# Attention's places in the first MoE's tiles spread wider, two more raw weight buffers, and the second MoE's first splits cut into pieces

## The chip, the cores and the metric

The kernel runs on one core of one Trainium2 chip. The metric is the device time of one execution in microseconds. Three runs of the kernel before gave 1160.42, 1161.3 and 1163.42 us; the median is 1161.3 us. Five engines work side by side, each through its own queue in order: TensorE (PE, with its weight loads PEld), VectorE (DVE), ScalarE (ACT), GpSimdE (POOL) and SyncE (SP, which here only issues DMAs).

## The reference

The input is a chunked attention (4 batches, 8 heads, 768 places, head width 64, chunks of 32 queries that see their own 32 places, 16 before, 8 behind and 8 memory places). Its output is 3072 rows of 512, and two mixtures of matrix products follow. All of it is float64 on the host or float32 on the chip.

```python
scores = scale * np.matmul(q_c, k_full.transpose(0, 1, 3, 2))
a = np.exp(scores - np.max(scores, axis=-1, keepdims=True))
a = a / (np.sum(a, axis=-1, keepdims=True) + 1e-09)
out[:, :, c_start:c_end] = np.matmul(a, v_full)
...
xn = x / rms * rms_g                       # first MoE, 512 -> 1536 -> 512
g = xn @ w_gate
h = g * (1.0 / (1.0 + np.exp(-g))) * (xn @ w_val)
x2 = h @ w_out
...
h = x2 @ w_in                              # second MoE, 512 -> 2048 -> 512
g = np.where(h >= 1, h, np.where(h <= -1, 0.0, (h + 1) ** 2 / 4))
y = g @ w_out
```

## The kernel before, in words

Every large product is done with each operand split into a high part and a low rest, both in a 32-bit matmul format, and three matmuls for each product (high x high, high x low, low x high). The rows are cut into six tiles of 512 (`TT`).

**Start.** Four units of attention (a unit is half of a pair of 128-row blocks) fill the first tile. `ORDER` writes that order out by hand: `s` scores, `m` and `e` softmax, `a` transposes of the exponentials, `A` their copy to SBUF, `v` product with the values, `n` division, `q`, `k`, `p`, `r` the row scaling, `x` transposes of the result, `c`, `d`, `g`, `o` the four steps that turn one raw weight into its two parts.

**First MoE, tiles t = 0 to 3**, one at a time. Each tile has twelve blocks f. A block is 12 matmuls of 512 columns for the gate (`proj_in` into `ps_g[0]`), 12 for the value (into `ps_g[1]`), 12 for the block before's output (`out1` into `ps_y`). After each of the three stands a slot, `slot(t, 3f)`, `slot(t, 3f+1)`, `slot(t, 3f+2)`: 36 slots in a tile. A slot may hold one step of attention for the tiles to come (`att_slot`: the table `plan` in tile 0, `plan2` and `plan3` in tiles 1 to 3, where a pair of units takes 11 slots), and some of the background work: in tile 0 `conv_w` and `load_w` (the 36 raw weights, 512 KB each, by way of the three buffers of `wst`), later `conv_step`, which makes the sums of weights that the second half needs. In the tiles of 1 and 2 `load_x` fetches the next tile's x (1 MB) at f = 9, and `split_x` splits it at f = 11. Slots 34 of tile 1 and 34 of tile 2 hold no attention. At f = 6 of tile 3 attention is over; its SBUF is given to the tile `y`, and `load_y` fetches tiles 4 and 5. From f = 8 on `x_steps`, twelve small groups of DVE and ACT work, one per slot, turn `y` into the operands of the pair.

In tile 0 PE and SP run in program order, and a scheduler places the instructions of ACT, DVE and POOL; from tile 1 on all engines run in program order. Attention's scores, transposes and products all go through one PSUM bank pair, `ps_a`.

**Pairs.** Tiles 4 and 5 in the first MoE, and all six tiles as three pairs in the second, are done with seven products instead of eight for a 2x2 block. `seven` is one such block of 42 matmuls: product 0 into bank A, product 1 into C, then ACT copies A to B (L891) and C to the tile `p5` (L892), product 2 adds into B, and so on; DVE adds `p5` and B into C (L899) and later into `p5` (L903). In the second MoE `proj2` runs eight such blocks for a pair, each followed by the clamp and square (`clamp`, `top`); then `Out.run` does the output product from splits (`split`: ACT's copy to a high part at L982, DVE's rest at L984, and a sum at L986). The splits of blocks 0 to 3 are made ahead, by `o2.ahead(g - 3)` behind blocks 3 to 6 of the projection. The first of the `x_steps` for the next pair, a DVE sum over 128x1024 (L812), is taken behind block 6.

Of the kernel before, what the change touches and what calls it, by code (L numbers as in the profile page):

```python
# [39 lines left out]
def tile_stream_attention_moe_moe2(  # L40
# [72 lines left out]
    raw, absd, f32s = [], [], []  # L113
# [413 lines left out]
    def step_x(pr, blk, ps):  # L527
# [4 lines left out]
        for kk in range(KK):  # L532
            nc.tensor.transpose(ps[:, 0, kk * P:(kk + 1) * P], x[blk][:, kk * P:(kk + 1) * P], ident)
        ps_t["x", pr, blk] = ps

    def part_X(pr, blk):
# [7 lines left out]
        rows = ps[:, 0, :].rearrange("p (k i) -> p k i", k=KK)  # L544
# [73 lines left out]
    for st in ORDER.split():  # L618
# [5 lines left out]
        if c in "savx":  # L624
            use[c, n] = free.pop(0)
            ps = slots[use[c, n]]
            if c == "x":
                step_x(n // 2, n % 2, ps)
# [31 lines left out]
        elif c == "d":  # L660
            conv_d()
            load_w(units1, 1)
# [15 lines left out]
    plan = {1: "s0", 3: "a0", 4: "v0", 7: "s1", 9: "a1", 10: "v1", 11: "r0", 14: "x0", 15: "x1"}  # L678

    plan2 = {0: "s0", 3: "a0", 4: "s1", 5: "v0", 6: "a1", 8: "v1", 11: "r0", 12: "x0", 13: "x1"}
    plan3 = {0: "s0", 3: "a0", 4: "s1", 5: "v0", 6: "a1", 7: "v1", 9: "r0", 10: "x0", 11: "x1"}

    def att_slot(t, s):
        if t == 0:
            o, r = divmod(s, 18)
            if r in plan:
                att_step(2 + o, plan[r])
            return  # L690

        if s == 34:
            return
        s += 36 * (t - 1)
        s -= (s > 34) + (s > 70)
# [6 lines left out]
    def att_step(pr, st):  # L702
# [3 lines left out]
        if st[0] == "x":  # L706
            step_x(pr, n, ps_a)
# [28 lines left out]
    def slot(t, s):  # L736
# [8 lines left out]
        else:  # L745
# [4 lines left out]
            conv_step(1 if s > 32 else PACE[(n - (n > 34) - (n > 70)) % 11] if n < 92 else 2.5)  # L750
# [74 lines left out]
    for t in range(NS):  # L825
# [3 lines left out]
        for f in range(F1):  # L829
            if 0 < t < NS - 1 and f == 9:  # L830
                load_x(t + 1)
# [9 lines left out]
            if t == NS - 1 and f == 6:  # L841
                att_only.close()
                right = ctx.enter_context(tc.tile_pool(name="right", bufs=1, side="right", reuse_waits="tile"))
                m2["y"] = right.tile([P, 2, KK, TT], F32, name="y")
                load_y(x_d[NS], x_d[NS + 1])
# [13 lines left out]
            slot(t, 3 * f + 2)  # L859
    for i in range(8, 14):  # L860
# [20 lines left out]
    banks, defer = [], []  # L881

    def seven(n, early):
# [7 lines left out]
        nc.scalar.activation(B, A, AF.Copy)  # L891
        nc.scalar.activation(p5, C, AF.Copy)  # L892
# [58 lines left out]
    class Out:  # L951
# [23 lines left out]
        def split(self, n):  # L975
# [9 lines left out]
            if p == 0:  # L985
                tt_(out=B11, in0=B12, in1=B11, op=ALU.add)  # L986

# [261 lines left out]
```

## Time and profile before

| | |
|---|---|
| median of three runs | 1161.3 us |
| the profiled execution | 1158.09 us |
| its span, first to last instruction | 1156.3 us |
| granted TensorE clock, mean | 0.989 |
| PE busy | 1125.6 us (97%) |
| DVE busy | 820.6 us (71%) |
| ACT busy | 617.3 us (53%) |
| bytes moved by DMA | 281.81 MB, 244 GB/s |

The span begins at the first instruction. In microseconds from there, the start takes until 35, tile 0 until 151, tile 1 until 272, tile 2 until 391, tile 3 until 503, the last pair of the first MoE until 676, and the three pairs of the second MoE the rest. A matmul's start tells more than its busy time, since matmuls are pipelined: the time from one start to the next is what the engine spends on one. In the timelines a row's brackets give the idle time of the engine just before it and what ended that; a wait for several things is put down to the one that came last by the trace's record, which may be the wrong one where that engine had long been done.

### The profile page before, as it was taken

What the parts mean: (1) busy time and instruction counts of PE and PEld (TensorE: products, weight loads), DVE (VectorE), ACT (ScalarE), POOL (GpSimd) and SP (SyncE); (2) the same over time, 40 slices, a digit from 0 to 9 for tenths busy, and PEclk for the clock granted to TensorE, in tenths of its full rate; (3) what the DMA queues carried; (4) which work ended last, traced back from release to release, by engine and by line L of the source; (5) the groups of instructions that cost most, each with busy time, mean ns of one, the idle gap of its engine ahead of it and who ended that gap; (6) DMA issues with size and microseconds to landing.
All of it is one profiled execution on the core that took longest, in us unless ns stands there. A gap on an engine that the chain in (4) does not pass through costs nothing.

```text
span 1156.3 us, 20945 instructions
## 1 busy us (share of the span) xinstructions
PE 1125.6 (97%) x7879; PEld 909.7 (79%) x7879; DVE 820.6 (71%) x1433; ACT 617.3 (53%) x1088; POOL 102.6 (9%) x152
## 2 busy tenths in 40 slices
PE   5899999999999999999999999999999999999998
PEld 4677788877788777887888888788887788887886
DVE  3887667767756666766676867897677887578855
ACT  3777665656565765534444634456444465344553
POOL 0200003213222222101110000000000000000000
PEclk7999999999999999999999999999999999999999
DMA  8776448998979887779997697756778666762564
GB/s 294 253 258 203 163 140 271 312 310 284 303 245 309 269 273 236 275 269 383 404 394 241 213 316 246 210 180 199 231 207 260 177 195 216 217 197 86 164 188 158
DMA packets 144212, 281.81 MB, mean 244 GB/s; under 512 B 15216, under 2 KB 65392, under 8 KB 142320
## 3 DMA queue, kind: packets, MB, share of 16 engines
q1 hardware_dynamic: 123664, 228.57, 60.7%
q0 software_dynamic: 12768, 43.52, 10.8%
q10 hardware_dynamic: 7680, 8.39, 2.1%
q8 instruction: 62, 1.02, 0.3%
q14 instruction: 38, 0.31, 0.1%
HBM read 201.26 MB, written 79.17 MB: 243 GB/s over the span
## 4 chain that ended last, share of the span: by engine, by line
PE 76%; DVE 8%; ACT 6%; DMA 6%; issue 3%; POOL 1%; SPq 0%; DVEq 0%; ACTq 0%; POOLq 0%
PE ps_y L1034 14%; PE ps_g L1034 11%; PE ps_g L557 6%; PE ps_g L559 5%; PE ps_g L558 5%; PE ps_g L872 3%; PE ps_b L872 3%; PE ps_b L874 3%; PE ps_b L873 3%; PE ps_g L874 3%; PE ps_g L873 3%; DMA w<-in_w_dram 3%; PE ps_y L557 3%; PE ps_y L558 3%; PE ps_y L559 3%
## 5 line engine op out<-in xcount | busy, mean ns | idle before, releaser
L557 PE MATMUL ps_g<-xh,wall 128*128 128x512 f32 x384 | 156.6, 408 | 3.2 <-ACT wall L152 3.2
L1034 PE MATMUL ps_y<-r,wo 128*128 128x512 f32 x672 | 156.2, 390 | 0.0
L558 PE MATMUL ps_g<-xl,wall 128*128 128x512 f32 x384 | 151.1, 394 | 0.4 <-DVE xl L652 0.4
L559 PE MATMUL ps_g<-xh,wall 128*128 128x512 f32 x384 | 151.3, 394 | 0.2 <-DVE wall L154 0.2
L1034 PEld LDWEIGHTS ps_y<-r,wo 128*128 128x128 f32 x672 | 125.7, 188 | 26.0
L984 DVE TENSOR_TENSOR r<-h,r 128x512 fp32r<-128x512 f32 x167 | 112.2, 689 | 44.0 <-ACT r L982 43.9
L935 ACT ACTIVATE t<-t,half 128x512 f32<-128x512 f32 x96 | 66.9, 720 | 128.4 <-DVE t L934 125.5
L982 ACT ACTIVATE r<-h 128x512 fp32r<-128x512 f32 x167 | 100.4, 624 | 56.2 <-DVE r L984 18.2
L1034 PE MATMUL ps_g<-r,wo 128*128 128x512 f32 x498 | 116.0, 390 | 0.0
L1034 PEld LDWEIGHTS ps_g<-r,wo 128*128 128x128 f32 x498 | 93.2, 188 | 19.4 <-DVE r L984 0.2
L557 PEld LDWEIGHTS ps_g<-xh,wall 128*128 128x128 f32 x384 | 72.8, 190 | 19.6 <-ACT wall L152 3.8
L559 PEld LDWEIGHTS ps_g<-xh,wall 128*128 128x128 f32 x384 | 72.7, 189 | 17.1 <-DVE wall L154 1.0
L558 PEld LDWEIGHTS ps_g<-xl,wall 128*128 128x128 f32 x384 | 73.0, 190 | 14.3 <-DVE xl L652 0.7
L872 PE MATMUL ps_g<-wall 128*128 128x512 f32 x198 | 78.4, 396 | 1.6 <-DVE ps_y L899 0.8
L872 PE MATMUL ps_b<-wall 128*128 128x512 f32 x202 | 79.2, 392 | 0.7 <-DVE ps_g L899 0.3
L873 PE MATMUL ps_b<-wall 128*128 128x512 f32 x202 | 78.6, 389 | 0.0
L874 PE MATMUL ps_b<-wall 128*128 128x512 f32 x202 | 78.6, 389 | 0.0
L557 PE MATMUL ps_y<-hh,wall 128*128 128x512 f32 x192 | 77.9, 406 | 0.0
L873 PE MATMUL ps_g<-wall 128*128 128x512 f32 x198 | 77.1, 390 | 0.0
L874 PE MATMUL ps_g<-wall 128*128 128x512 f32 x198 | 77.1, 389 | 0.0
L558 PE MATMUL ps_y<-hl,wall 128*128 128x512 f32 x192 | 75.2, 392 | 0.0
L559 PE MATMUL ps_y<-hh,wall 128*128 128x512 f32 x192 | 74.9, 390 | 0.0
(199 smaller groups left out, 2086.7 us busy)
## 6 DMA issues: line engine op xcount, KB each, us to landing
wo<-w2o_d SPq DMA_DIRECT2D x88, 512.0 KB, 3.4
wall<-w2p_d SPq DMA_DIRECT2D x168, 256.0 KB, 2.9
wall<-w1p_d SPq DMA_DIRECT2D x84, 256.0 KB, 5.9
w<-in_w_dram SPq DMA_DIRECT2D x36, 512.0 KB, 4.6
w<-in_w_dram POOLq DMA_DIRECT2D x32, 512.0 KB, 5.7
k_in<-in_k_dram SPq DMA_DIRECT2D x48, 256.0 KB, 4.9
wo<-w1o_d SPq DMA_DIRECT2D x21, 512.0 KB, 3.5
v_in<-in_v_dram SPq DMA_DIRECT2D x40, 260.0 KB, 4.3
```

The lines of the kernel that those rows point to most:

```text
L557: nc.tensor.matmul(ps, wh, xh, start=start, stop=False)
L558: nc.tensor.matmul(ps, wh, xl, start=False, stop=False)
L559: nc.tensor.matmul(ps, wl, xh, start=False, stop=stop)
L872: nc.tensor.matmul(bank, wh, xh, start=st, stop=False, skip_group_check=True)
L873: nc.tensor.matmul(bank, wh, xl, start=False, stop=False, skip_group_check=True)
L874: nc.tensor.matmul(bank, wl, xh, start=False, stop=kk == 1, skip_group_check=True)
L935: nc.scalar.activation(s, s, AF.Square, scale=0.5, bias=half)
L982: nc.scalar.activation(r[:, 0], src, AF.Copy)
L984: tt_(out=r[:, 1], in0=src, in1=r[:, 0].bitcast(F32), op=ALU.subtract)
L1034: nc.tensor.matmul(bank[p][m], a, b, start=s0, stop=s1, skip_group_check=True)
```

## The change

It has four parts.

- **Tile 0's weights.** Two more raw buffers (`w64s`) are cut out of the `xn` tile, which tile 0 needs only once attention's third pair is transposed. Of the first 15 raw weights every fourth and fifth goes there; one more load is issued in the start.
- **Attention's places.** In tile 0 the two pairs no longer stand at the same places of two halves of 18 slots; one table gives all 18 places, with two slots or more between `a` and its `v`, and `x0` and `x1` two slots apart. In tiles 1 and 2 slots 33 and 34 (36 + 34 and 36 + 35 in tile 2) hold no attention instead of one slot each, so everything behind them stands one or two slots later; `plan2` scales a pair (`r0`) at 10 instead of 11.
- **Order of loads.** `load_x` stands behind the slot at f = 9 instead of ahead of it; the giving away of attention's SBUF and `load_y` stand behind slot 3f+2 of f = 6 instead of 3f.
- **Second MoE.** The first splits are no longer made behind a block but in pieces inside the next one (`pieces`, `due`): ACT's copy behind the bank copy L891, DVE's rest ahead of the sum L899, DVE's sum behind it. The first of the `x_steps` goes there too, behind the first clamp.

```diff
     def load_w(units, n):
         for _ in range(n):
             if units:
                 dst, key, src = units.pop()
-                w64 = wst.tile([P, 1024], U32, tag="w64", name="w64")
+                i = 3 * F1 - 1 - len(units)
+                if i == 3:
+                    spare.append(xs.tile([P, 2, 1024], U32, tag="xn", name="w64s"))
+                if i < 15 and i % 5 > 2:
+                    w64 = spare[0][:, i % 5 - 3]
+                else:
+                    w64 = wst.tile([P, 1024], U32, tag="w64", name="w64")
                 nc.sync.dma_start(w64, src)
...
             conv_d()
-            load_w(units1, 1)
+            load_w(units1, 1 if n else 2)
...
-    plan = {1: "s0", 3: "a0", 4: "v0", 7: "s1", 9: "a1", 10: "v1", 11: "r0", 14: "x0", 15: "x1"}
-    plan2 = {0: "s0", 3: "a0", 4: "s1", 5: "v0", 6: "a1", 8: "v1", 11: "r0", 12: "x0", 13: "x1"}
+    plan = {
+        2: (2, "a0"), 4: (2, "v0"), 5: (2, "s1"), 7: (2, "a1"), 9: (2, "v1"), 11: (2, "r0"), 12: (2, "x0"), 14: (2, "x1"),
+        16: (3, "s0"), 19: (3, "a0"), 21: (3, "v0"), 22: (3, "s1"), 24: (3, "a1"), 26: (3, "v1"), 29: (3, "r0"),
+        30: (3, "x0"), 32: (3, "x1"),
+    }
+    plan2 = {0: "s0", 3: "a0", 4: "s1", 5: "v0", 6: "a1", 8: "v1", 10: "r0", 12: "x0", 13: "x1"}
...
-        if s == 34:
+        s += 36 * (t - 1)
+        if s in (33, 34, 70, 71):
             return
-        s += 36 * (t - 1)
-        s -= (s > 34) + (s > 70)
+        s -= 2 * (s > 34) + 2 * (s > 71)
...
-            if 0 < t < NS - 1 and f == 9:
-                load_x(t + 1)
...
             slot(t, 3 * f)
-            if t == NS - 1 and f == 6:
-                att_only.close()
-                ...
-                load_y(x_d[NS], x_d[NS + 1])
+            if 0 < t < NS - 1 and f == 9:
+                load_x(t + 1)
...
             slot(t, 3 * f + 2)
+            if t == NS - 1 and f == 6:
+                att_only.close()
+                ...
+                load_y(x_d[NS], x_d[NS + 1])
...
         nc.scalar.activation(B, A, AF.Copy)
+        due(0)
         nc.scalar.activation(p5, C, AF.Copy)
...
         product(7 * n + 3, A, False)
+        due(1)
         tt(out=C, in0=p5, in1=B, op=ALU.add)
+        due(2)
         done11 = early(A)
+        due(3)
...
+        def pieces(self, n):
+            if not 0 <= n < self.L:
+                return
+            p, k, B11, B12, B21, B22 = self.block(n)
+            r = m2["ring"][n % len(m2["ring"])]
+            later2[0].append(lambda: nc.scalar.activation(r[:, 0], B11, AF.Copy))
+            later2[1].append(lambda: tt_(out=r[:, 1], in0=B11, in1=r[:, 0].bitcast(F32), op=ALU.subtract))
+            later2[2].append(lambda: tt_(out=B11, in0=B12, in1=B11, op=ALU.add))
...
             proj2(G2 * pr + g)
-            o2.ahead(g - 3)
+            if g < G2 - 1:
+                o2.pieces(g - 3)
...
             if g == 6 and xq:
-                xq.pop(0)()
+                later2[3].append(xq.pop(0))
```

How the instructions stand on their engines, at three places. In all of them the program's line numbers of the changed kernel are 6 to 28 higher than before.

First, PE in block f = 0 and 1 of tile 0, before (`ps_g_111` is `ps_g[0]`, `ps_g_112` is `ps_g[1]`, `ident,e` the transposes `a0` of unit 4):

```order
L557 MATMUL ps_g_111<-xh,wall 128x512
L558 MATMUL ps_g_111<-xl,wall 128x512
L559 MATMUL ps_g_111<-xh,wall 128x512
L437 MATMUL ps_a<-ident,e 128x128 x4
L557 MATMUL ps_g_112<-xh,wall 128x512
```

and now:

```order
L564 MATMUL ps_g_112<-xl,wall 128x512
L565 MATMUL ps_g_112<-xh,wall 128x512
L443 MATMUL ps_a<-ident,e 128x128 x4
L563 MATMUL ps_g_111<-xh,wall 128x512
L564 MATMUL ps_g_111<-xl,wall 128x512
```

The transposes stood between the gate and the value product of f = 1; they stand now behind the value product of f = 0, 12 matmuls earlier. On ACT the same stretch read before (`tu<-w` is step `c` of a raw weight, `wall<-tu` step `g`, `e<-e` the exponential that the transposes read, with the table load ahead of it):

```order
L152 ACTIVATE wall<-tu 128x512
L128 ACTIVATE tu<-w_587 128x512
L837 ACT_TABLE_LOAD
L837 ACTIVATE s<-ps_g_111 128x512
L152 ACTIVATE wall<-tu 128x512
L432 ACT_TABLE_LOAD
L432 ACTIVATE e<-e 128x512
L128 ACTIVATE tu<-w_669 128x512
```

and now:

```order
L158 ACTIVATE wall<-tu 128x512
L134 ACTIVATE tu<-w64s 128x512 x2
L841 ACT_TABLE_LOAD
L841 ACTIVATE s<-ps_g_111 128x512
L158 ACTIVATE wall<-tu 128x512
L438 ACT_TABLE_LOAD
L438 ACTIVATE e<-e 128x512
L134 ACTIVATE tu<-w_670 128x512
```

Two raw weights instead of one are taken up ahead of the exponential; the one that came behind it (`w_669`) is now the second `w64s`.

Second, SP at f = 9 of tile 1, before (`xn<-x_d` is `load_x`, `v_in` the values of unit 13, `w1p_d` a store of summed weights):

```order
L202 DMA w1p_d_141<-wgv 128x2x256
L202 DMA w1p_d_141<-s_2878 128x2x256
L552 DMA xn<-x_d_119 128x2048
L392 DMA v_in<-in_v_dram 128x520 x2
L202 DMA w1p_d_142<-wgv 128x2x256
```

and now:

```order
L208 DMA w1p_d_141<-wgv 128x2x256
L208 DMA w1p_d_141<-s_2873 128x2x256
L398 DMA v_in<-in_v_dram 128x520 x2
L558 DMA xn<-x_d_119 128x2048
L208 DMA w1p_d_142<-wgv 128x2x256
```

The two loads of the values stand ahead of the load of x.

Third, ACT in the second MoE, pair 0, around the start of block 4, before (`half` marks the square of `clamp`, `r<-h` the split's high part, `ps_g_112<-ps_y_705` the bank copy, the last row but one the copy to `p5`):

```order
L935 ACTIVATE t_7243<-t_7243,half 128x512
L982 ACTIVATE r_7244<-h 128x512
L891 ACTIVATE ps_g_112<-ps_y_705 128x512
L892 ACTIVATE t_7237<-ps_g_111 128x512
L935 ACTIVATE t_7238<-t_7238,half 128x512
```

and now:

```order
L950 ACTIVATE t_7233<-t_7233,half 128x512
L902 ACTIVATE ps_g_112<-ps_y_706 128x512
L1010 ACTIVATE r_7239<-h 128x512
L904 ACTIVATE t_7234<-ps_g_111 128x512
L950 ACTIVATE t_7235<-t_7235,half 128x512
```

The bank copy has come ahead of the split's copy. The same exchange stands in blocks 4 to 7 of each of the three pairs.

## Rows read from the trace of the kernel before

**Rows 1.** The page: span, busy time of each engine with its share and instructions.

```profile
span 1156.3 us, 20945 instructions
PE 1125.6 (97%) x7879; PEld 909.7 (79%) x7879; DVE 820.6 (71%) x1433; ACT 617.3 (53%) x1088; POOL 102.6 (9%) x152
```

**Rows 2.** Waits of PE, whole span: who for whom: us in total, times, longest.

```profile
PE ps_g L557 <- ACT wall L152: 3.2, 2, 1.6
PE ps_a L453 <- ACT aT L443: 2.2, 4, 0.7
PE ps_a L533 <- ACT x_nat L546: 1.8, 4, 0.6
```

**Rows 3.** Timeline of PE, tile 0: start us, us, engine line op tiles xcount [idle].

```profile
36.90 0.40 PE L557 MATMUL ps_g<-xh,wall 128*128 128x512 f32 x1
41.46 0.39 PE L559 MATMUL ps_g<-xh,wall 128*128 128x512 f32 x1
46.61 0.50 PE L557 MATMUL ps_g<-xh,wall 128*128 128x512 f32 x1 [1.59 <-ACT wall L152]
58.42 0.50 PE L557 MATMUL ps_g<-xh,wall 128*128 128x512 f32 x1 [1.56 <-ACT wall L152]
61.02 0.63 PE L558 MATMUL ps_g<-xl,wall 128*128 128x512 f32 x1
61.45 0.63 PE L559 MATMUL ps_g<-xh,wall 128*128 128x512 f32 x1
```

**Rows 4.** Stretches of tile 0: busy by engine, granted clock, DMA share, GB/s.

```profile
30.00:36.00 6.00, 5.20 (x85) 2.94 (x83) 5.46 (x11) 4.40 (x11) 0.69 (x1) 0.77 0.27 90
52.00:58.00 6.00, 4.87 (x22) 3.69 (x20) 4.21 (x13) 3.02 (x9) 2.18 (x3) 1.00 0.93 304
58.00:64.00 6.00, 5.42 (x76) 3.66 (x76) 4.88 (x9) 3.44 (x6) 0.00 (x0) 0.72 0.88 315
```

**Rows 5.** Timeline of ACT, tile 0, columns as in rows 3.

```profile
41.01 1.28 ACT L432 ACT_TABLE_LOAD   x1
42.30 0.63 ACT L432 ACTIVATE e<-e 128x512 f32<-128x512 f32 x1
56.25 0.66 ACT L128 ACTIVATE tu<-w 128x512 f32<-128x512 f32 x1 [1.40 <-DMA w<-in_w_dram]
```

**Rows 6.** Timeline of SP, end of tile 1.

```profile
244.96 1.13 SPq L552 DMA_DIRECT2D xn<-x_d  x1
246.18 1.24 SPq L392 DMA_DIRECT2D v_in<-in_v_dram  x2
```

**Rows 7.** DMA issues of 244 to 248 us: xcount, KB each, us to landing.

```profile
v_in<-in_v_dram SPq DMA_DIRECT2D x2, 260.0 KB, 7.3
```

**Rows 8.** Timeline of PE, end of tile 1.

```profile
253.67 0.35 PE L453 MATMUL ps_a<-v_in,aT 64*32 64x65 f32 x16 [2.35 <-ACT wgv L197]
256.00 0.63 PE L559 MATMUL ps_g<-xh,wall 128*128 128x512 f32 x1
```

**Rows 9.** Timeline of DVE, tile 3.

```profile
469.84 1.23 DVE L812 TENSOR_TENSOR y<-y 128x1024 f32<-128x1024 f32 x1 [0.83 <-DMA y<-x_d]
473.77 0.69 DVE L849 TENSOR_TENSOR s<-s,ps_g 128x512 f32<-128x512 f32 x1 [2.37 <-PE ps_g L559]
```

**Rows 10.** Timeline of ACT, second MoE, pair 0.

```profile
716.28 0.62 ACT L982 ACTIVATE r<-h 128x512 fp32r<-128x512 f32 x1
716.80 0.58 ACT L891 ACTIVATE ps_g<-ps_y 128x512 f32<-128x512 f32 x1
726.74 0.58 ACT L891 ACTIVATE ps_y<-ps_b 128x512 f32<-128x512 f32 x1
```

**Rows 11.** Timeline of PE, second MoE, pair 0.

```profile
716.92 0.39 PE L874 MATMUL ps_g<-wall 128*128 128x512 f32 x1
717.43 0.50 PE L872 MATMUL ps_g<-wall 128*128 128x512 f32 x1
...
750.62 0.50 PE L872 MATMUL ps_g<-wall 128*128 128x512 f32 x1 [0.38 <-DVE ps_y L899]
```

More of the change, by code (lines that the diff above doesn't have):

```diff
@@ L112, in tile_stream_attention_moe_moe2 @@
     w1 = {}
-    raw, absd, f32s = [], [], []
+    raw, absd, f32s, spare = [], [], [], []
     def load_w(units, n):
@@ L532, in step_x @@
         for kk in range(KK):
-            nc.tensor.transpose(ps[:, 0, kk * P:(kk + 1) * P], x[blk][:, kk * P:(kk + 1) * P], ident)
+            nc.tensor.transpose(ps[:, kk * P:(kk + 1) * P], x[blk][:, kk * P:(kk + 1) * P], ident)
         ps_t["x", pr, blk] = ps
@@ L543, in part_X @@
             xn = x_t[pr][blk].rearrange("p (k i) -> p k i", k=KK)
-        rows = ps[:, 0, :].rearrange("p (k i) -> p k i", k=KK)
+        rows = ps.rearrange("p (k i) -> p k i", k=KK)
         for kk in range(KK):
@@ L627, in tile_stream_attention_moe_moe2 @@
             if c == "x":
-                step_x(n // 2, n % 2, ps)
+                step_x(n // 2, n % 2, ps[:, 0])
             else:
@@ L686, in att_slot @@
         if t == 0:
[L687 to L690, printed above, removed]
-        if s == 34:
+            if s in plan:
+                att_step(*plan[s])
             return
         s += 36 * (t - 1)
-        s -= (s > 34) + (s > 70)
+        if s in (33, 34, 70, 71):
+            return
+        s -= 2 * (s > 34) + 2 * (s > 71)
         for pr in range(4, 2 * NTT):
@@ L706, in att_step @@
         if st[0] == "x":
-            step_x(pr, n, ps_a)
+            step_x(pr, n, ps_a[:, 0])
             part_X(pr, n)
@@ L749, in slot @@
             n = s + 36 * (t - 1)
-            conv_step(1 if s > 32 else PACE[(n - (n > 34) - (n > 70)) % 11] if n < 92 else 2.5)
+            conv_step(1 if s > 32 else PACE[(n - 2 * (n > 34) - 2 * (n > 71)) % 11] if n < 94 else 2.5)
             for fn in after:
@@ L840, in tile_stream_attention_moe_moe2 @@
             slot(t, 3 * f)
-            if t == NS - 1 and f == 6:
-                att_only.close()
-                right = ctx.enter_context(tc.tile_pool(name="right", bufs=1, side="right", reuse_waits="tile"))
-                m2["y"] = right.tile([P, 2, KK, TT], F32, name="y")
-                load_y(x_d[NS], x_d[NS + 1])
+            if 0 < t < NS - 1 and f == 9:
+                load_x(t + 1)
             proj_in(ps_g[1], w1[("v", f)])
@@ L859, in tile_stream_attention_moe_moe2 @@
             slot(t, 3 * f + 2)
+            if t == NS - 1 and f == 6:
+                att_only.close()
+                right = ctx.enter_context(tc.tile_pool(name="right", bufs=1, side="right", reuse_waits="tile"))
+                m2["y"] = right.tile([P, 2, KK, TT], F32, name="y")
+                load_y(x_d[NS], x_d[NS + 1])
     for i in range(8, 14):
@@ L879, in tmp2, with due @@
         return m2["t"][m2["n"] % len(m2["t"])]
-    banks, defer = [], []
+    banks, defer, later2 = [], [], {k: [] for k in range(4)}
+    def due(k):
+        while later2[k]:
+            later2[k].pop(0)()
     def seven(n, early):
@@ L986, in split @@
                 tt_(out=B11, in0=B12, in1=B11, op=ALU.add)
+        def pieces(self, n):
+            if not 0 <= n < self.L:
+                return
+            p, k, B11, B12, B21, B22 = self.block(n)
+            assert p == 0
+            r = m2["ring"][n % len(m2["ring"])]
+            later2[0].append(lambda: nc.scalar.activation(r[:, 0], B11, AF.Copy))
+            later2[1].append(lambda: tt_(out=r[:, 1], in0=B11, in1=r[:, 0].bitcast(F32), op=ALU.subtract))
+            later2[2].append(lambda: tt_(out=B11, in0=B12, in1=B11, op=ALU.add))
         def ahead(self, n):
```

## The prediction

> **What bounds the kernel now.** I read the page first: PE is busy for 1125.6 of 1156.3 us [rows 1], so nothing is gained unless PE waits less or runs fewer matmuls at a low clock; the change adds and takes away no matmul, it only moves them. Second the timeline of PE, for what one matmul of 512 columns costs where nothing waits: 20 starts lie between 36.90 and 41.46 us, 0.228 us each [rows 3]. Where the profile shows the lower level of TensorE's clock, 1.2 GHz instead of 2.4, two starts lie 0.43 us apart (61.02, 61.45) [rows 3], so a matmul there loses 0.20 us. Third the waits of PE: a reader is to see that few are long, and that behind the start the long ones lie in the first MoE's tiles: weights (3.2 us), the copy of the transposed exponentials (2.2), the evacuation of transposed x (1.8) [rows 2], and one for the values (2.35) [rows 8]. Last the second MoE, where no wait in the list is long but a small one repeats, by the starts of PE [rows 11] beside ACT's queue [rows 10]. The four edits each name one of these places, so I price them one by one.
>
> **Tile 0.** PE stood still 1.59 us before the value product of f = 1 and 1.56 us before that of f = 2, both for the high part of a weight [rows 3]. ACT had idled for the raw weight: at 56.25 us it had just waited 1.40 us for the load, and the high part that PE wanted was queued behind that [rows 5]. Two more buffers put the loads of units 3 and 4 where the start ends: the DMA share there is 0.27, in 52 to 58 us 0.93 [rows 4]. One load more (512 KB) fits into that hole: at the 304 GB/s of the full stretch it takes 1.7 us, and 6 us at 0.27 leave 4.4. Every later unit is asked for earlier by one or two, since its buffer is no longer the one just emptied. So I let both waits go (3.2), with them the slow start of the matmul behind each (0.1 each, 0.50 instead of 0.39 long, [rows 3]) and the run at the lower clock that followed the second: 58 to 64 us have 0.72 of full clock [rows 4], seven matmuls 0.43 apart, 1.4 us lost. Of the four waits for the transposed exponentials [rows 2] three lie in this tile, where `v` stood one slot behind its `a`; 2.2 less the longest 0.7 is 1.5, and with two slots between, 24 matmuls or 5.5 us, all of it goes. Sum 6.3.
>
> On the other side stands `a0` of unit 4, now 12 matmuls earlier. PE is done with f = 0 at 41.46 + 0.23 = 41.69 us. The exponential ended at 42.30 + 0.63 = 42.93 [rows 5], and it is now one conversion later in ACT's queue (two `w64s` instead of one `w`), 0.66 long [rows 5] and some 0.5 of it before the next one can start (as from 716.28 to 716.80, [rows 10]), so 43.5; PE waits 1.8 to 1.9 us. Queued behind it on PE are the gate and value products of f = 1, which then find their weights ready, so the wait takes the place of the first weight wait. Bounds of the new wait: 1.2, if the second conversion slides behind the exponential, to 3.6, if it draws the lower clock for eight matmuls as the wait at 58.42 did. I take 1.9. Tile 0: -6.3 + 1.9 = -4.4, bounds -6 and 0.
>
> The trace shows the table load ahead of the exponential at 41.01, 1.28 us long, and the exponential 1.29 us behind its start [rows 5]. The Trainium skill (ScalarE: Activation LUTs, "What ACT_TABLE_LOAD costs") puts 1.38 us of draining on top of the load at each switch of set. By the rule the new wait would be 3.3 instead of 1.9, the total 1.4 us later; by the row there is no such time here, and I go by the row.
>
> **Tile 1's end.** Before `v1` of unit 13 PE idled 2.35 us [rows 8]. The list names ACT for it, but the values were issued at 246.18, behind the load of x at 244.96 [rows 6], and took 7.3 us [rows 7], until 253.5: that is when PE went on. With the load of x behind, the values go out 1.2 us earlier and have 1 MB less ahead of them. At 304 GB/s [rows 4] 1 MB is 3.4 us, so they land at 253.5 - 1.2 - 3.4 = 248.9; PE wants them at 253.67 - 2.35 = 251.3. So the idle goes, and with it the run at the lower clock behind it (one of its rows, at 256.00, is 0.63 long [rows 8]; there are seven such, 1.4 us): 2.35 + 1.4 = 3.75. Bounds: -4.1, with the restart, and 0 if the queue is served so that the order does not matter. What is late next is the load of x: the values now ahead of it are 520 KB, 1.7 us, and it is split only behind the value product of f = 11, over 36 matmuls or 8 us after this place.
>
> **`r0` a slot earlier, x0 and x1.** Four waits of 1.8 us in all [rows 2], where `x1` follows one slot behind `x0` and ACT has the scaling, a table load and the exponential ahead of the evacuation. Taking the scaling (two rows) out of that slot frees about 1.2 us of ACT, more than any of the four; one of them lies in the last pair, which `plan3` leaves as it was. I take -1.1, bounds -1.6 and +0.5.
>
> **Tile 3.** Attention ends two slots later (12 matmuls twice, 5.5 us), and `load_y` with it. DVE's first sum over `y` already waited 0.83 us for it, at 469.84 [rows 9]. It will wait to 469.8 + 5.5 = 475.3 in PE's time. Queued behind it on DVE is, after background work, the product with the value bank (L849): at 473.77 now, 0.69 long [rows 9], it comes to 475.3 + 1.23 = 476.5 and ends at 477.2. Who waits for it is PE, which begins to write that bank anew 24 matmuls after it was full, 473.8 + 5.5 = 479.3. The cover is 2.1 us, so I cost it at 0; bounds 0 and +3, if a transfer takes longer by its own length (1 MB, 3.4 us).
>
> **Second MoE.** In blocks 4 to 7 of each pair ACT's split (716.28) stood ahead of the bank copy (716.80) and held it for 0.52 [rows 10], and PE, which adds into that bank, went from 716.92 to 717.43 [rows 11]: 0.51 instead of 0.23, with 0.11 more for the start behind it, 0.39. The same pair of rows stands twelve times: 4.7. In the seventh block of the first two pairs DVE's sum over 128x1024, L812, 1.23 us long [rows 9], made the sum behind it late and PE idle 0.38 [rows 11]; with restart 0.64, twice, 1.3. Together 6.0. In exchange the split sits between the bank copy and the copy to `p5`. That one waits for product 1 anyway; a block is 42 matmuls, product 1 ends 1.36 us after product 0, and the bank copy (0.58) plus the split (0.62 at most) [rows 10] fit in 1.36 with 0.16 to spare. DVE's part fits the time it idles in a block. The wide sum now stands between the clamp and the sum into `p5`, with one product, 1.36 us, of cover behind; it is 0.4 late there at most. I take -6.0; bounds -6.4 and -2.
>
> **The sum.** -4.4 - 3.75 - 1.1 + 0 - 6.0 = -15.3 us, against the profiled execution's 1158.1 us: 1142.8. That execution is 3.2 us under the median of the runs, 1161.3, which is what the new median is compared with: 1161.3 - 15.3 = 1146.0. The last pair of the first MoE gets one background step less to do; its order against the products moves by a place, and I count nothing for it, plus or minus 0.5.
>
> **Rivals.** (1) *Tile 0 gains nothing.* DMA is full there (0.93) [rows 4], so loads asked for earlier only wait longer in the queue, the second weight wait comes back and the new wait on `a0` stays. For: 0.93, and ACT's queue stays in order behind a late load. Against: the hole in 30 to 36 us, which moves whole loads out of the full stretch. Price +4.4: 1150.4. The Trainium skill (DMA: Bandwidth & Descriptors, "Issuing engines are not separate DMA queues") has all queues share the same 16 engines; the share in rows 4 fits it, and by it this is the case that I would fear. (2) *Attention's delay in the tiles reaches PE*: `y` lands later than 477.4, or `x0` and `x1` at the tile's edge meet the split of the next tile on ACT. For: DVE waits there already [rows 9]. Against: 2.1 us of cover. Price 1.1 lost and 3 to 5 more: 1150 to 1152. (3) *The pieces do not do it*: the split delays the copy to `p5`, DVE's sum comes late and product 5 waits as product 2 did. For: only 0.16 us of room on ACT. Against: DVE's sum waits for product 2, not for `p5`. Price 4.7: 1150.7. (4) *Slower*: the wait on `a0` at 41.7 us leaves PE at the lower clock, as in the start, and 0.20 us are lost per matmul. It decides from 15.3 / 0.20, 77 matmuls on, that is over two blocks of tile 0; at 90 matmuls the time is 1164. For: granted clock 0.77 up to 36 us [rows 4]. Against: the wait of 1.59 at 46.61 was followed by full clock.
>
> **How the numbers follow.** My forecast has 0.62 (1143 to 1149 by its own terms), rival 1 0.18, rival 2 0.10, rival 3 0.06, rival 4 0.04. Two rivals together give 1154; so I take 1142 to 1154, which leaves out rival 4 and the tails, about 2 in 10. About 0.3%, 3.5 us, is what a measurement of this kernel can tell from no change. Faster means under 1157.8: all of the forecast, of rivals 1 and 3 and nearly all of 2, 0.93; the same takes 0.04, slower 0.03 from rival 4.
>
> **What would show it.** Right: no idle of over 0.5 us for a weight before the value products of f = 1 and 2, and one of 1.5 to 2.2 before the transposes of unit 4; no idle before `v1` of unit 13, the values landing before 251; bank copies in blocks 4 to 7 of the second MoE 9.6 us apart (42 times 0.228) where they now stand 9.94 apart [rows 10]; PE's waits in the list down by about 8 us. Wrong: PE waiting for the value bank in tile 3, waits for L899 in the second MoE, or rows 0.43 apart for more than ten matmuls.

## The result, and the profile after

The changed kernel took 1141.47 us (median of four runs, 1140.51 to 1142.45), the kernel before beside it 1162.36 (four runs, 1160.42 to 1163.58): a ratio of 0.982, 95% interval 0.980 to 0.984. Two further sets of runs gave 0.984 (0.981 to 0.986) and 0.985 (0.983 to 0.987). Over all sets the medians are 1141.85 (12 runs) and 1160.5 (67 runs), 18.7 us apart. The forecast was 1146.0 with a range of 1142 to 1154: the direction was right, the gain was put at 15.3 us, and the first median lay 0.5 us under the range.

The page of the changed kernel, against [rows 1]:

```profile
span 1139.3 us, 20945 instructions
PE 1117.0 (98%) x7879; PEld 909.7 (80%) x7879; DVE 817.8 (72%) x1433; ACT 617.3 (54%) x1088; POOL 103.9 (9%) x152
```

The same instructions, 17.0 us less span. To see where, I take the start of the same matmul of 512 columns at each stage's edge in both traces (a matmul's number in the order of all such matmuls is the same in both, 4500 of them), and the time between. The edge between tile 0 and tile 1 is taken twelve matmuls into tile 1; the second MoE ends with the start of the last matmul. Three profiles are of the changed kernel; for before, each stage has five to eight, since experiments that leave a stage alone are samples of it too.

| stage | before, profile read | before, mean (lowest to highest, profiles) | after, mean of 3 | difference of means | forecast |
|---|---|---|---|---|---|
| start | 35.46 | 35.18 (34.14 to 36.21, 7) | 34.94 | -0.2 | 0 |
| tile 0 | 118.79 | 119.63 (117.48 to 124.10, 7) | 116.05 | -3.6 | -4.4 |
| tiles 1 to 3 | 348.85 | 349.58 (348.85 to 350.17, 5) | 342.77 | -6.8 | -4.85 |
| last pair, first MoE | 197.74 | 198.22 (197.74 to 199.18, 7) | 197.11 | -1.1 | 0 |
| second MoE | 448.85 | 448.86 (448.75 to 448.95, 8) | 443.07 | -5.8 | -6.0 |

The second MoE repeats to 0.2 us and came as forecast. Tile 0 is what varies most from run to run. Against these means the miss is in tiles 1 to 3 and the last pair. Against the one execution that the forecast was read from, the stages fell by 15.8 us, not 17.5.

The marks that the prediction named. In tile 0 no weight wait is left; the new wait of `a0` is there, on PE:

```profile
39.98 0.39 PE L565 MATMUL ps_g<-xh,wall 128*128 128x512 f32 x1
42.40 0.66 PE L443 MATMUL ps_a<-ident,e 128*128 128x128 f32 x4 [2.03 <-ACT e L438]
43.77 0.63 PE L563 MATMUL ps_g<-xh,wall 128*128 128x512 f32 x1
44.20 0.63 PE L564 MATMUL ps_g<-xl,wall 128*128 128x512 f32 x1
```

and on ACT ahead of it:

```profile
39.78 0.62 ACT L158 ACTIVATE wall<-tu 128x512 fp32r<-128x512 f32 x1
40.42 1.28 ACT L438 ACT_TABLE_LOAD   x1
41.71 0.63 ACT L438 ACTIVATE e<-e 128x512 f32<-128x512 f32 x1
```

2.03 us against the 1.8 to 1.9 forecast, and behind it eight starts lie 0.43 apart, 1.6 us more. That second part is not in every execution: in the third profile of the changed kernel the same wait, also 2.03 us, was followed by starts 0.23 apart, at full granted clock.

```profile
44.32 0.66 PE L443 MATMUL ps_a<-ident,e 128*128 128x128 f32 x4 [2.03 <-ACT e L438]
45.05 0.39 PE L564 MATMUL ps_g<-xl,wall 128*128 128x512 f32 x1
45.28 0.39 PE L565 MATMUL ps_g<-xh,wall 128*128 128x512 f32 x1
```

A wait that the prediction did not name is new as well: `s1` (L413) waits for its bank twice in tile 0, 0.52 and 0.94 us in this profile, 0.40 and 2.01 in the third.

The stretches of tile 0 in the first profile (columns as in [rows 4]) show both sides: the lower clock behind the wait, and the loads that come earlier, 397 GB/s at 48 to 54 us:

```profile
42.00:48.00 6.00, 5.60 (x20) 4.52 (x21) 5.22 (x10) 5.92 (x11) 2.46 (x4) 0.72 0.96 343
48.00:54.00 6.00, 5.88 (x86) 4.30 (x84) 3.75 (x10) 3.66 (x7) 1.54 (x3) 1.00 1.02 397
```

At the end of tile 1 the values are issued ahead of x on SP, where [rows 6] have them behind, and land 6.4 us later (the DMA issues of that stretch, as in [rows 7]); PE takes them without idling where [rows 8] show 2.35 us:

```profile
239.59 2.25 SPq L398 DMA_DIRECT2D v_in<-in_v_dram  x2
241.89 1.32 SPq L558 DMA_DIRECT2D xn<-x_d  x1
```

```profile
v_in<-in_v_dram SPq DMA_DIRECT2D x2, 260.0 KB, 6.4
```

```profile
247.00 0.86 PE L459 MATMUL ps_a<-v_in,aT 64*32 64x65 f32 x64
```

In tile 3 DVE now waits 5.49 us for `y`, against 0.83 in [rows 9], and PE has no idle time in that stretch: the cover of 2.1 us that the prediction counted on held.

```profile
463.59 1.23 DVE L818 TENSOR_TENSOR y<-y 128x1024 f32<-128x1024 f32 x1 [5.49 <-DMA y<-x_d]
464.73 0.68 DVE L850 TENSOR_TENSOR s<-s,ps_g 128x512 f32<-128x512 f32 x1
```

In the second MoE's pair 0, ACT's bank copies stand 9.52 us apart (before 9.94, [rows 10]), with the split between the bank copy and the copy to `p5`:

```profile
705.06 0.58 ACT L902 ACTIVATE ps_g<-ps_y 128x512 f32<-128x512 f32 x1
705.58 0.61 ACT L1010 ACTIVATE r<-h 128x512 fp32r<-128x512 f32 x1
706.19 0.60 ACT L904 ACTIVATE t<-ps_g 128x512 f32<-128x512 f32 x1
...
714.58 0.58 ACT L902 ACTIVATE ps_y<-ps_b 128x512 f32<-128x512 f32 x1
```

PE's waits in the whole list add up to 17.8 us against 24.5: 6.7 less, where about 8 had been named.

### The profile page after: what moved, and what is told of

Its sections match the earlier page's. It is cut to its first block, busy times and chain, and to the rows that moved or that the text cites. A ratio compares the mean times of both kernels' runs of the same rounds, so it can differ in the third digit from the quotient of the medians.

```text
span 1139.3 us, 20945 instructions
## 1 busy us (share of the span) xinstructions
PE 1117.0 (98%) x7879; PEld 909.7 (80%) x7879; DVE 817.8 (72%) x1433; ACT 617.3 (54%) x1088; POOL 103.9 (9%) x152
## 3 DMA queue, kind: packets, MB, share of 16 engines
q8 instruction: 62, 1.02, 0.4%
## 4 chain that ended last, share of the span: by engine, by line
PE 89%; DMA 5%; ACT 2%; DVE 2%; issue 1%; SPq 0%; POOL 0%; DVEq 0%; ACTq 0%
PE ps_y L1060 14%; PE ps_g L1060 11%; PE ps_g L563 7%; PE ps_g L564 7%; PE ps_g L565 7%; PE ps_y L563 4%; PE ps_b L880 4%; PE ps_b L878 4%; PE ps_b L879 4%; PE ps_g L878 3%; PE ps_g L880 3%; PE ps_g L879 3%; PE ps_y L564 3%; PE ps_y L565 3%; DMA wall<-w1p_d 2%; PE ps_y L880 2%
## 5 line engine op out<-in xcount | busy, mean ns | idle before, releaser
L999 DVE TENSOR_TENSOR r<-h,r 128x512 fp32r<-128x512 f32 x155 | 103.8, 687 | 44.2 <-ACT r L997 44.2
L997 ACT ACTIVATE r<-h 128x512 fp32r<-128x512 f32 x155 | 92.9, 625 | 55.9 <-DVE r L999 17.5
```

The lines of the kernel that those rows point to most:

```text
L997: nc.scalar.activation(r[:, 0], src, AF.Copy)
L999: tt_(out=r[:, 1], in0=src, in1=r[:, 0].bitcast(F32), op=ALU.subtract)
```

## The experiments

### How far single executions lie apart: the two kernels again

Both unchanged.

> The kernel before, once more, with a new profile. Theory A (the base): the execution that I read, 1158.1 us, was one of the short ones; the start and tile 0 vary from run to run with the clock, and an execution of 1161 to 1163 us has its 3 to 5 us more ahead of 151 us, in PE's waits and in matmuls 0.43 us apart; the second MoE is the same in all. Theory B (chance): executions spread evenly from 1158 to 1164, a second profile is no longer than the first, and where it is longer the extra lies anywhere, behind 151 us too. Ratio to the kernel before: 1.000 by both.

> The changed kernel once more. Theory A: the change takes away waits at which the clock can fall, so its runs lie closer together than those of before (2 us between lowest and highest instead of 5), at 1140 to 1143, ratio 0.982 to 0.984. Theory B: it is worth the 17.0 us between the two profiled executions, ratio 0.985 to 0.986, and its runs spread as widely as those of before.

Before: 1160.13 us (12 runs, 1155.74 to 1165.19), ratio 0.999 (0.998 to 1.001). After: 1141.64 (4 runs, 1139.46 to 1143.49), ratio 0.984, as its theory A had it; its four runs span 4.0 us, where A had 2. The new profile of before was of its longest run, 1165.19, 7.1 us above the one that I had read. By the stages, +0.4 is in the start, +5.3 in tile 0, +1.3 in tile 1 and nothing behind it. So theory A holds as to place: nearly all that varies lies in waits of the kinds that the change takes away. It fails as to the base: over 67 runs the median is 1160.5, and the profile read lay 2.4 under it, not 3.2. The waits of PE in this profile, to compare with [rows 2]:

```profile
PE ps_g L557 <- ACT wall L152: 5.9, 2, 3.2
PE ps_a L453 <- DMA v_in<-in_v_dram: 4.1, 2, 3.8
...
PE ps_a L453 <- ACT aT L443: 3.8, 3, 2.2
PE ps_a L533 <- ACT x_nat L546: 1.8, 4, 0.6
```

The weight waits are 5.9 us instead of 3.2, the copy of the exponentials 3.8 instead of 2.2; the wait for the evacuated x is the same 1.8. How a copy comes to be 2.2 us late is seen on ACT and PE at 131 us:

```profile
130.74 0.67 ACT L128 ACTIVATE tu<-w 128x512 f32<-128x512 f32 x1 [3.03 <-DMA w<-in_w_dram]
131.43 1.28 ACT L837 ACT_TABLE_LOAD   x1
132.72 0.60 ACT L837 ACTIVATE s<-ps_g 128x512 f32<-128x512 f32 x1
133.22 0.59 ACT L443 ACTIVATE aT<-ps_a 128x512 f32<-128x512 f32 x1
```

```profile
131.29 0.39 PE L559 MATMUL ps_g<-xh,wall 128*128 128x512 f32 x1
133.86 0.86 PE L453 MATMUL ps_a<-v_in,aT 64*32 64x65 f32 x64 [2.18 <-ACT aT L443]
```

ACT waits 3.03 us for a raw weight, and the copy that PE needs is queued behind it. The list blames the copy; the cause is a load three instructions ahead.

### One part alone: the second MoE's pieces, the order of the loads

```diff
         nc.scalar.activation(B, A, AF.Copy)
+        due(0)
         nc.scalar.activation(p5, C, AF.Copy)
...
+        due(1)
         tt(out=C, in0=p5, in1=B, op=ALU.add)
+        due(2)
         done11 = early(A)
+        due(3)
```

> Only the second MoE's splits in pieces; everything else as before. If the term is right: twelve bank copies 9.56 us apart instead of 9.94, no wait for the sum over y in the seventh blocks, 5.8 to 6.0 us less in the stretch from 703 us to the end, ratio 0.9948, and the same in any run whatever the start does. Rival (part of it was only taken elsewhere, by the weights' DMA): 2 us or less, ratio above 0.998, new waits for wall in the second MoE.

1153.67 us (6 runs), ratio 0.994 (0.992 to 0.997). From the first matmul of the second MoE to the last it is 443.11 us, where before has 448.86: 5.75 less, as in the changed kernel. The term is right and stands by itself.

```diff
-            if 0 < t < NS - 1 and f == 9:
-                load_x(t + 1)
...
             slot(t, 3 * f)
+            if 0 < t < NS - 1 and f == 9:
+                load_x(t + 1)
```

> Only the load of x behind the slot at f = 9 of tiles 1 and 2, and so behind the values of attention; everything else as before. If the term is right: the values land before 251 us, PE's idle of 2.35 us at 253.7 and the seven matmuls 0.43 apart behind it are gone, 3.75 to 4.1 us less by the trace, ratio 0.9965. Rival: the order does not matter to when the values land, and the wait went in the changed kernel because attention stands one slot later there: then less than 1 us here, ratio above 0.999.

1155.25 us (9 runs), ratio 0.996 (0.994 to 0.997); tiles 1 to 3 take 345.52 us against 349.58, 4.1 less. The order alone does it, so the rival is out:

```profile
242.40 2.43 SPq L392 DMA_DIRECT2D v_in<-in_v_dram  x2
244.88 0.74 SPq L552 DMA_DIRECT2D xn<-x_d  x1
```

The values land 6.2 us behind their issue (at 248.9, which the prediction had for them, and 249.5), and PE does not idle before its product with them.

### Tile 0: the buffers and the places

> Before, with the two more raw buffers and the one load more in the start, and nothing else. Theory A (the buffers take the weight waits): the waits of PE for the high part of a weight ahead of the value products of f = 1 and 2, 1.6 us each in the execution that was read and 2.6 and 3.2 in the second, go, with seven to ten matmuls at the lower clock; 4 to 6 us less, ratio 0.995 to 0.997, and the runs lie closer together than before's 1156 to 1166. Rival 1 of the prediction (DMA is full there, earlier asking gains nothing): under 1 us, ratio above 0.999.

> The changed kernel without the two raw buffers and the extra load. Theory A: weight waits of 1.5 to 3.2 us are back ahead of the value products of f = 1 or 2, and the wait of 2.0 us for a0 of unit 4 stays or shrinks to 1.2; 3 to 6 us longer than the changed kernel, ratio 0.987 to 0.989. Rival (the places do it, not the buffers): within 1 us of the changed kernel, 0.983 to 0.985.

Before plus the two buffers:

```diff
+                if i < 15 and i % 5 > 2:
+                    w64 = spare[0][:, i % 5 - 3]
+                else:
+                    w64 = wst.tile([P, 1024], U32, tag="w64", name="w64")
...
-            load_w(units1, 1)
+            load_w(units1, 1 if n else 2)
```

1157.25 us (12 runs), ratio 0.997 (0.995 to 0.999). The weight waits of 1.6 each shrink to 0.34 and 0.70 us, both in f = 1, but the runs lie hardly closer together (within 7.7 us, before's beside them within 8.6):

```profile
46.20 0.50 PE L563 MATMUL ps_g<-xh,wall 128*128 128x512 f32 x1 [0.34 <-ACT wall L158]
46.54 0.40 PE L564 MATMUL ps_g<-xl,wall 128*128 128x512 f32 x1
47.64 0.50 PE L565 MATMUL ps_g<-xh,wall 128*128 128x512 f32 x1 [0.70 <-DVE wall L160]
```

The changed kernel without the buffers (the same edit undone): 1146.14 us (6 runs), ratio 0.988 (0.986 to 0.990), 4 to 5 us longer than with them; a wait of 2.87 us is back at 57.5 us, now ahead of scores. What holds those up is again a raw weight: ACT waits 2.59 us for it at 54.9, DVE 2.14 at 56.1 for the high part that ACT makes of it, and the division (L480), on which the scores wait, is queued behind that on DVE. Rival 1 of the prediction (DMA is full, nothing is gained) is out from both sides.

```diff
-        2: (2, "a0"), 4: (2, "v0"), 5: (2, "s1"), 7: (2, "a1"), 9: (2, "v1"), 11: (2, "r0"), 12: (2, "x0"), 14: (2, "x1"),
+        3: (2, "a0"), 4: (2, "v0"), 7: (2, "s1"), 9: (2, "a1"), 10: (2, "v1"), 11: (2, "r0"), 14: (2, "x0"), 15: (2, "x1"),
...
```

(the old places; the second pair's likewise)

> The changed kernel with attention's old places in tile 0 (a0 at slot 3, v one slot behind its a), all else as changed. Theory A (a0 one slot early costs 2.03 us and eight matmuls 0.43 apart behind it, 3.6; the two slots between a and v save 1.5 to 3): the wait for the exponential at 42 us is gone, waits for the copy aT of 0.4 to 2 us are back; 0 to 2 us shorter than the changed kernel, ratio 0.982 to 0.984. Rival (the wider places are what tile 0 gained): 3 us longer or more, ratio 0.9865 or above.

1144.01 us (4 runs), ratio 0.986 (0.984 to 0.988), some 2 us longer than the changed kernel: neither number, on the rival's side. The trace agrees as to which waits come and go: no wait for the exponential at 42 us, but three more for the copy of the exponentials than the changed kernel has. It does not show the 2 us in tile 0, which takes 115.81 us here and 116.05 in the changed kernel's mean; what this profile has more is in the last pair, behind a wait of 1.66 us for a weight. So what the wider places gained in tile 0 is not shown.

```profile
PE ps_a L459 <- ACT aT L449: 2.5, 4, 1.1
```

> Before, with tile 0's part of the change alone: the two raw buffers, the extra load and the new places of attention in tile 0. Theory A (the parts add up): the stretch from the first instruction to tile 1 is 155.1 us in the mean of the four profiles that have before's tile 0, and 150.7 in the two of the changed kernel; 4.4 us less, ratio 0.996, and runs within 4 us of each other. Rival (the part is larger in the runs than in the profiles, and is what the forecast missed): 7 us less or more, ratio 0.994 or below.

This is before with tile 0's part alone (the buffers, the extra load and the new places, as in the change): 1156.23 us (11 runs, 1153.87 to 1159.01; a twelfth, of 5468.59, is left out, and nothing here explains it), ratio 0.997 (0.995 to 0.998). That is 4.2 us less than before beside it, theory A, with the runs 5 us apart where 4 had been expected.

### Places that avoid the new wait

```diff
-        2: (2, "a0"), 4: (2, "v0"), 5: (2, "s1"), 7: (2, "a1"), 9: (2, "v1"), 11: (2, "r0"), 12: (2, "x0"), 14: (2, "x1"),
-        16: (3, "s0"), 19: (3, "a0"), 21: (3, "v0"), 22: (3, "s1"), 24: (3, "a1"), 26: (3, "v1"), 29: (3, "r0"),
-        30: (3, "x0"), 32: (3, "x1"),
+        3: (2, "a0"), 5: (2, "v0"), 7: (2, "s1"), 9: (2, "a1"), 11: (2, "v1"), 12: (2, "r0"), 14: (2, "x0"), 16: (2, "x1"),
+        18: (3, "s0"), 20: (3, "a0"), 22: (3, "v0"), 24: (3, "s1"), 26: (3, "a1"), 28: (3, "v1"), 29: (3, "r0"),
+        31: (3, "x0"), 33: (3, "x1"),
```

> The changed kernel with other places in tile 0: a0 at slot 3 again, and every step of attention two slots behind the one before that uses the same bank, s1 too, which now stands one slot behind v0. Theory A: the wait of 2.03 us for the exponential goes with the low clock behind it (3.6), and the waits of s1 for the bank (0.52 and 0.94) go (1.8 with restarts); 4 to 5 us shorter than the changed kernel, about 1137, ratio 0.979 to 0.981. Rival: the weight for the value product of f = 1 is not ready when the wait ahead of it is gone, and takes its place: under 1.5 us shorter, ratio above 0.982.

> The kernel with every step of tile 0's attention two slots apart, again, beside the changed kernel on the same chip: 2 to 3 us shorter than the changed kernel (1139.9 against 1141.5 to 1142.4 in other runs), ratio to before 0.980 to 0.982. Rival: the difference was between runs, ratio the same within 0.001.

> The changed kernel a third time, beside the three others: 18 to 20 us less than before, ratio 0.983 to 0.984; start and tile 0 within 1.5 us of the other two profiles, everything behind tile 0 within 1 us.

The first time 1139.89 us (4 runs), ratio 0.983 (0.981 to 0.985); the second 1141.74 (5 runs), 0.984 (0.982 to 0.987), beside the changed kernel's 1142.33 (4 runs), 0.985 (0.983 to 0.987), on the same chip. The gain of 4 to 5 us did not come; 0.6 us cannot be told from nothing. The wait for `a0` is gone, but weight waits of 0.34 and 0.70 stand in f = 1, and in the second profile another exponential is late, that of `a1` in slot 9. PE, and ACT ahead of it:

```profile
68.30 0.66 PE L443 MATMUL ps_a<-ident,e 128*128 128x128 f32 x4 [2.35 <-ACT e L438]
```

```profile
65.65 0.66 ACT L134 ACTIVATE tu<-w64s 128x512 f32<-128x512 f32 x1 [2.10 <-DMA w64s<-in_w_dram]
66.33 1.28 ACT L438 ACT_TABLE_LOAD   x1
67.62 0.63 ACT L438 ACTIVATE e<-e 128x512 f32<-128x512 f32 x1
```

Again a raw weight that has not landed, with attention's step queued behind it. The third profile of the changed kernel has a wait of 2.0 us at another place of tile 0 (`s1` behind its bank, L413 for DVE's L486); behind tile 0 it lies up to 2.2 us above the others, 1.5 of it a wait for `wall` in the last pair, where 1 had been expected.

```diff
-        7: (2, "s1"), 9: (2, "a1"), 11: (2, "v1"), 12: (2, "r0"), 14: (2, "x0"), 16: (2, "x1"),
+        7: (2, "s1"), 10: (2, "a1"), 12: (2, "v1"), 13: (2, "r0"), 14: (2, "x0"), 16: (2, "x1"),
```

> The changed kernel with other places in tile 0: as in the kernel with every step two slots apart, but a1 of unit 5 three slots behind its s1 (s1 7, a1 10, v1 12, r0 13, x0 14, x1 16). Theory A (a1 waited 0.4 and 2.4 us there for an exponential that stood on ScalarE behind a late raw weight): that wait is gone, 1 to 2 us shorter than with every step two slots apart, 1138 to 1140, ratio 0.980 to 0.982. Rival: x0, one slot behind r0, waits for the scaled rows instead, and the time is that of the changed kernel, 0.983 to 0.985.

1143.37 us (4 runs), ratio 0.986 (0.984 to 0.988). The rival: `a1` does not wait, `x0` does, one slot behind the scaling.

```profile
80.79 0.65 PE L539 MATMUL ps_a<-ident,x_nat 128*128 128x128 f32 x4 [1.56 <-ACT x_nat L526]
```

No version beat the changed kernel by more than the measurement can tell.

### Tiles 1 to 3 and the last pair

> Before, with the places of tiles 1 to 3 alone: r0 at 10, two empty slots instead of one, attention and the load of y two slots later. Theory A (this is the term that I sized at 1.1 and that is larger): the four waits for the evacuation of x are gone or one of 0.3 is left, the waits for the sums at 527, 547 and 605 us too, tiles 1 to 3 are 2.5 to 3 us shorter and the last pair about 1; ratio 0.996 to 0.9975. In addition attention's later slots bring the value product of f = 9 in tile 1 behind the landing of its values, up to 4 us more: then 0.993. Rival (sized right): 1 us less, ratio 0.999 or above.

Before with the places of tiles 1 to 3, the background's pace and the place of `load_y`, all as in the change: 1155.62 us (8 runs), ratio 0.997 (0.995 to 0.999). Tiles 1 to 3 take 346.43 us against 349.58, 3.15 less; the last pair 197.05 against 198.22, 1.2 less. That is the term that I had at 1.1, though not all of the 3.15 belongs to it: at the wait for the values PE idles 2.0 us here, against 3.3 in the mean of before's five profiles. Of the four waits ahead of `x1` one of 0.26 is left. Alone, the four parts gave 6.8 (pieces), 5.3 (loads), 4.2 (tile 0) and 4.9 us, 21 together, where the whole gave 18.7; the overlap at the wait for the values is about 1 us of that, the rest is not placed. The next two split the places, with one profiled run each.

```diff
-    plan2 = {0: "s0", 3: "a0", 4: "s1", 5: "v0", 6: "a1", 8: "v1", 11: "r0", 12: "x0", 13: "x1"}
+    plan2 = {0: "s0", 3: "a0", 4: "s1", 5: "v0", 6: "a1", 8: "v1", 10: "r0", 12: "x0", 13: "x1"}
```

> Before, with the row scaling of tiles 1 and 2 one slot earlier (10 instead of 11) and nothing else. Theory A (the scaling ahead of it made the evacuation of x0 late): the waits for the evacuation of x ahead of x1, 0.57, 0.61 and 0.34 us, are gone, the one of 0.31 in the last pair stays; 1.9 us less in tiles 1 to 3, and the three waits for the sums at 527, 547 and 605 us stay. Rival (the empty slots did it): the waits are as in before.

```diff
-        if s == 34:
-            return
+        if s in (33, 34, 70, 71):
+            return
-        s -= (s > 34) + (s > 70)
+        s -= 2 * (s > 34) + 2 * (s > 71)
```

(and `load_y` and the background's pace, `n < 94` and two places for each gap, with it; the pace is a line of the change that its diff above leaves out)

> Before, with the empty slots of tiles 1 to 3, the background's pace that goes with them and the load of y two slots later, and r0 as before. Theory A: the three waits for the sums at 527, 547 and 605 us go, since the background's steps stand one place earlier against the seven products; the waits ahead of x1 stay at 0.3 to 0.6; the wait for the values in tile 1 stays, shorter by up to 1 us. Rival: the sums come late because of the scaling, and their waits stay.

With `r0` alone (1155.59 us, one run) the list of PE's waits has, against 1.8 us and four times in [rows 2], and with the pair's wait for DVE's sum left as it was (0.3 in before too):

```profile
PE ps_b L872 <- DVE ps_g L899: 0.3, 1, 0.3
PE ps_a L533 <- ACT x_nat L546: 0.3, 1, 0.3
```

With the slots alone (1157.45 us, one run):

```profile
459.71 0.66 PE L533 MATMUL ps_a<-ident,x_nat 128*128 128x128 f32 x4 [0.26 <-ACT x_nat L546]
```

as the only wait ahead of `x1`, and no wait for L899 in the last pair. With `r0` alone, tiles 1 to 3 take 347.56 us, 2.0 less, where 1.9 had been expected. But the expectation that the waits ahead of `x1` need the earlier `r0` fell: either edit takes the three in tiles 2 and 3 (all but 0.15 us of one, with `r0` alone). Neither takes the one of attention's last pair, 0.31 us in before: it is 0.31 with `r0` alone, 0.26 with the slots alone and 0.26 in the changed kernel. How the empty slots do it was not traced. The waits in the last pair of the first MoE belong to the slots, the pace and `load_y`, as expected; which of these three does it is not shown. DVE in before and then in the changed kernel, at the sum (L899, now L912) for which PE waited 0.31 us until 528.17:

```profile
526.82 0.69 DVE L139 SCALAR_TENSOR_TENSOR g_b<-w,g_b 128x512 uint32<-128x512 uint32 x1
527.43 0.69 DVE L899 TENSOR_TENSOR ps_g<-t,ps_b 128x512 f32<-128x512 f32 x1
```

```profile
515.49 0.42 DVE L197 TENSOR_TENSOR late<-tu 128x256 f32<-128x256 f32 x1
516.12 0.70 DVE L912 TENSOR_TENSOR ps_g<-t,ps_b 128x512 f32<-128x512 f32 x1 [0.22 <-PE ps_b L880]
```

Before, the sum stood behind background work that had begun too late; now DVE is free 0.22 us before the sum may start.

## Why the prediction was off, point by point

**Second MoE, right.** -6.0 forecast, -5.8 in the trace, alone and with the rest.

**Tile 1's end, right.** -3.75 forecast, bounds -4.1 and 0; the order of the loads alone gave 4.1 by the trace. The price was read from an execution in which the wait was short: 2.35 us there, 3.8 in the second profile.

**Tile 0, near in its sum by luck, not in its terms.** -4.4 forecast, -3.6 in the profiles' means (-3.8 with the start), about 4 measured alone. The wait on `a0` cost 3.6 (2.03 and the lower clock), the end that I had named for it, in two of three profiles, and 2.0 in the third, where I took 1.9; the waits of `s1` for its bank, 1.5 to 2.4 us, I had not seen at all. What they replaced was larger than I had read, since the waits for weights and copies in before are 5.4 us in one profile and 9.7 in another. The errors offset each other. The Trainium skill (ScalarE: Activation LUTs, "What ACT_TABLE_LOAD costs") would have had the wait at 3.3; the trace has the exponential 1.29 us behind its table load again and the wait at 2.03.

**`r0`, x0 and x1: the step that failed.** "One of them lies in the last pair, which `plan3` leaves as it was. I take -1.1, bounds -1.6 and +0.5." The mechanism held: with `r0` alone the three waits went, and the one in attention's last pair stayed. The size was wrong. The three are 1.5 us of idling (0.57, 0.61 and 0.34), and I took 1.1. And idling is not their price: the matmul behind a wait also starts 0.16 us late (above, 131.29 to 133.86 is 2.57 us, of which 0.23 is a matmul and 2.18 idle), and the start behind that comes another 0.1 late. I had counted both in the second MoE and neither here; with them the three were worth 2.3. Measured: 2.0 less in tiles 1 to 3 with `r0` alone, and 2.7 in the changed kernel (6.8 less the 4.1 of the loads), where the one profile of the loads alone has longer waits of this kind than the others. That the empty slots take the same three waits, I had not seen: I had read them only as a delay of attention.

**The last pair: the second step that failed.** "I count nothing for it, plus or minus 0.5." I gave no reason for the nothing. Three waits for DVE's sum stood in the trace, at 528.17, 547.60 and 605.09 us, only the first of them in the list of waits:

```profile
527.48 0.39 PE L874 MATMUL ps_b<-wall 128*128 128x512 f32 x1
528.17 0.50 PE L872 MATMUL ps_b<-wall 128*128 128x512 f32 x1 [0.31 <-DVE ps_g L899]
528.51 0.40 PE L873 MATMUL ps_b<-wall 128*128 128x512 f32 x1
547.14 0.39 PE L874 MATMUL ps_g<-wall 128*128 128x512 f32 x1
547.60 0.50 PE L872 MATMUL ps_y<-wall 128*128 128x512 f32 x1
```

By the distance of the starts, less the 0.23 of a matmul, they are 0.46, 0.23 and 0.23 us, and 0.1 more each for the start behind (528.17 to 528.51 is 0.34), 1.2 together. The empty slots, with the pace and `load_y`, cleared all three; at the first of them DVE's rows above show the background's steps earlier against the sum. I had priced only what moves into a place, not what it moves out of the way of. Measured: -1.1 in the changed kernel, -1.2 with the places alone. A wait for a weight (`wall`) in the same stage varies between profiles, up to 0.9 us in before's and 1.5 in the changed kernel's.

**The base: the third step that failed.** "That execution is 3.2 us under the median of the runs, 1161.3, which is what the new median is compared with: 1161.3 - 15.3 = 1146.0." This takes it that those 3.2 us are still there in the changed kernel. By the stages, before's profiles lie 1.8 us in the mean above the one that I read: 0.8 in tile 0, 0.7 in tiles 1 to 3, 0.5 in the last pair, less 0.3 in the start. What tile 0 and tiles 1 to 3 have of it are waits of the kinds that the change takes away; in the last pair it is the wait for `wall`, which it leaves. Against the execution that I read, the changed kernel's mean is 15.8 us less, where I had 15.3; against the mean of before's profiles, 17.5. That 15.8 is so near 15.3 is luck again: against that execution the start and tile 0 had been put 1.1 too high, tiles 1 to 3 and the last pair 1.2 and 0.6 too low. Subtracted from the execution that it was read from, my sum was 1142.8, 1 us above the 1141.85 measured. Of the 4.15 us between that and 1146.0, 0.8 is the median of three runs, which lay that much above that of 67; 1.8 is what before's other profiles have beyond the one that I read; 0.4 is in the terms; for the last 1.1 three profiles are too few, and its cause stays open.

**The range.** The lower bounds of my terms add up to -18.6 us: with every one at its best end the time would still have been 1142.7, because two terms had no room for a gain that I had not looked for.

**The rivals.** 1 (buffers gain nothing) is refuted by two kernels; the Trainium skill (DMA: Bandwidth & Descriptors, "Issuing engines are not separate DMA queues") made me fear it, and what the traces add is that the shared engines still had rate to give, 397 GB/s against 304; 3 (the pieces) is refuted by one, 2 by the trace in tile 3, while at the tile's edge, its other place, PE does wait for the split of the next tile's x, but only 0.22 us, at 379.9; 4 began as described in two of three profiles, a lower clock behind the `a0` wait, and ended after eight matmuls instead of the 77 from which it would have decided.

## What to carry to other kernels

Price a wait of PE by the distance of two starts, not by its idle time, and look at the rows behind it for the lower clock. Where an engine works in order, the wait that a list puts down to a copy can be a load some instructions ahead of the copy; giving that load a buffer more was worth more here (about 4 us) than moving the copy (2 at the most), and moving the copy often only showed the next step that is queued behind a load. And read a profile's variable stages from several executions, and subtract a gain from the execution that it was read from: here the stages behind tile 0 repeat to 1.7 us or less while tile 0 spans 6.6.

## What the runs showed of the hardware

The lower clock came behind several of PE's waits and not behind others. Behind 2.03 us of idling at 42.4 us eight starts lay 0.43 apart (granted clock 0.72 in 42 to 48 us), but none behind the same 2.03 us at 44.3 in the third profile (1.00 in 44 to 50); behind 2.18 at 133.9 in the second profile of before seven; in the first, behind 1.56 at 58.4 seven, but behind 1.59 at 46.6 none [rows 3]. So in these rows the length of the wait alone does not tell whether the lower clock follows. DMA moved 397 GB/s in the changed kernel's stretch of 48 to 54 us, with a share of 1.02, where before had 304 at 0.93 in 52 to 58 [rows 4]: a stretch that is called full by its share was not at its rate.
